# A fused attention and two-MLP kernel: wo's whole weights in three buffers, late conversions a step earlier, GpSimd's subtractions on VectorE

## The chip, the cores and the metric

The kernel runs on one core of one Trainium2 chip. The metric is the device time of one execution in microseconds, the median of several runs. TensorE (PE) does the matmuls, VectorE (DVE) and ScalarE (ACT) the elementwise work, GpSimd (POOL) a few subtractions, and SyncE (SP) issues nearly all DMAs.

## The reference

Three stages, all in float32:

```
attention   4 x 8 heads, 768 positions, 64 wide, in chunks of 32 queries:
            softmax(0.125 * q k^T) v over 8 memory keys, 16 to the left, the chunk, 8 to the right
moe         x = heads side by side (3072 x 512);  x = ((x @ w_a) * (x @ w_b)) @ w_out     d_ff 1536
moe2        h = x @ w_in (1024 wide);  solu = h * softmax(h)
            ln = (solu - mean) / sqrt(var + 1e-6) * g_ln;  result = ln @ w_out
```

The weights of both MLPs arrive as 64-bit floats and are turned into 32-bit ones on the chip.

## The kernel before, in words

**Products.** Every float32 value is split into a high part in the fast 32-bit format and a low part, and a product is three matmuls (low by high, high by low, high by high). So for each operand ScalarE copies the high part and VectorE subtracts it from the value to get the low part (`op_hi` and `op_lo`, line 691, for operands of the third products; `w2_hi` and `w2_lo`, line 816, for the second MLP's weights; `x1_hi` and `x1_lo`, line 575; `h_hi` and `h_lo`, line 927). Many products are done by a seven-product scheme (Strassen-Winograd's), which needs sums and differences of blocks of weights and of inputs (`s1_sums`, `wo_sums`, `t1_sum`, `t_sum`, `w2_sub`, `h_sums`).

**Order of time.** The 3072 tokens are six blocks of 512. (1) Block 0: attention, and conversion of the first MLP's weights; (2) block 1, with the attention of later blocks between; the weights' high and low parts and sums go to DRAM (`wsa`, `wsb` for the gates, `wod` for halves of w_out, `woz` for its whole values). (3) Two super-blocks of two blocks each (`sb` 0 and 1): a loop over 12 units `f` of d_ff, seven products a step, with ring buffers for `wsa` and `wsb` (`ring_load`), and then 36 *third products* (`third`), which multiply by pieces of w_out of 256 KB, six of them held at a time (`piece_load`, line 660). (4) The second MLP in 12 pairs of tiles of 128 tokens (`h_...`, `soft_...`, `t_mm`, `o_mm`).

**What sets the order.** TensorE, VectorE and ScalarE run in the order in which the program is written. Work beside the products is put at ticks: `at(t, fn, ...)` files a call, and each product ends with `tick()`, which makes the calls filed for it. `when(sb, f, k)` is the tick of product `k` in step `f`; `f = NF1` (12) is the stretch of third products. The orders of SyncE's and GpSimd's queues are made by the framework's planner from its own simulation; each queue then waits in order, so an instruction that waits holds up all behind it.

**Around the change.** Whole values of w_out (`woz`) are loaded for each of six pairs `p` of units into `wo_z()`, two rows of one tile (`r[3][:, 4:6]`, the same rows for all six), turned into sums (`wo_sums`), split (`wo_hi`, `wo_lo`) and stored as `wos` (`wo_store`, line 629); `wo_load` is line 615. The first two weights' whole values and their DRAM copies come from `wo_keep` (the addition is line 477). The last heads' attention runs in *pairs* of 128 queries between the products of super-block 0: `pair_load` (lines 288 and 292) loads values, q and k, `pair_S` makes scores, `pair_V` (line 360) the value products after a copy on ScalarE (line 345). In super-block 1 the 16 units of the second MLP's weights are loaded, converted (`w2_load`, `w2_abs`, `w2_low`, `w2_range`, `w2_sign`, `w2_add`), and split; seven of w_out's eight units are stored and placed again later (`w2_store`, `w2_place`); the w_in units are combined by `w2_sub` on GpSimd (line 824) in the stretch of third products. `h_sums` (line 901, GpSimd) makes the sums of a tile pair's inputs. Results of the first MLP go to DRAM by `out3` and `out3x` (lines 732 and 737).

The lines that give the shared tile and GpSimd's subtraction:

```
    def wo_z():
        return held["r"][3][:, 4:6]
...
        nc.gpsimd.tensor_tensor(out=w2_z(o), in0=w2_z(a), in1=w2_z(b), op=ALU.subtract)
```

Of the kernel before, what the change touches and what calls it, by code (L numbers as in the profile page):

```python
# [8 lines left out]
F32 = mybir.dt.float32  # L9
# [46 lines left out]
def fused_kernel(  # L56
# [552 lines left out]

    def wo_z():  # L610
        return held["r"][3][:, 4:6]

    def wo_load(p):
        for i in range(2):
            nc.sync.dma_start(wo_z()[:, i], woz[p + i * HF])

    def wo_sums():
        z = flat(wo_z()).rearrange("p (i c) -> p i c", i=4)
        for o, a, b, op in (
            (3, 1, 3, ALU.add),  # L620
            (1, 0, 1, ALU.subtract),
            (0, 3, 0, ALU.subtract),
            (2, 2, 0, ALU.subtract),
        ):
            nc.vector.tensor_tensor(out=z[:, o], in0=z[:, a], in1=z[:, b], op=op)

    def wo_store(p, h):
        t = flat(wo_z() if h else chunk(14).bitcast(F32))
        nc.sync.dma_start(wos[p][:, h].rearrange("p n c -> p (n c)"), t)

    def wo_hi(p):
        nc.scalar.copy(flat(chunk(14)), flat(wo_z()))

    def wo_lo(p):
        z = flat(wo_z())
# [12 lines left out]
    def piece_load(q):  # L648

        i, p = (0, q) if q < HF else order[q - HF]  # L650
        src = {
            0: lambda: wod[p][:, :, 0:256],
            1: lambda: wod[p + HF][:, :, 0:256],
            2: lambda: wos[p][:, :, 0],
            3: lambda: wos[p][:, :, 3],
            4: lambda: wos[p][:, :, 2],
            5: lambda: wos[p][:, :, 1],
            6: lambda: wod[p + HF][:, :, 256:512],
        }[i]()
        nc.sync.dma_start(wo_piece(q).bitcast(F32), src)  # L660

    def op_chunk(k):

        if k < 0:
            return chunk(27 + (k + HF) % 2)
        if k < 24:
            n = (17, 20, 27, 29, 15, 16, 21, 18, 19, 22, 23, 28)[k % 12]
        else:
            n = ((17, 20, 27, 29, 18, 19, 23, 28), (17, 20, 27, 29, 21, 22, 23, 28))[cur["sb"]][k % 8]
        return chunk(n)  # L670
# [218 lines left out]
    def h_sums(j):  # L889
# [5 lines left out]
        for i, a, b, op in (  # L895
# [508 lines left out]
    for t, i in zip((17, 20, 22, 25, 27, 29, 32), (0, 1, 2, 5, 3, 4, 6)):  # L1404
        at(when(0, NF1, t - 2), x1_hi, i)
        at(when(0, NF1, t), x1_lo, i)
    for sb in range(NSB):
        for p in range(HF):
# [3 lines left out]
            if p < HF - 1:  # L1412
# [17 lines left out]
            ),  # L1430
        )[sb]
        for p in range(HF):
            a, b = order.index((2, p)), order.index((1, p))
            for (f, k), (fn, *i) in zip(places[p], (
                (t_sum, 2, p), (op_hi, a), (op_hi, b), (op_lo, a), (op_lo, b), (t_sum, 4, p)
            )):
                at(when(sb, f, k), fn, *i)
        for p in range(HF):
            at(when(sb, NF1, 8 + p), t_sum, 3, p)
        for k in range(12, 6 * HF):  # L1440
            at(when(sb, NF1, k - 6), op_hi, k)
            at(when(sb, NF1, k - 5), op_lo, k)

    at(when(1, 0, 0), w2_buffers)
    for i in range(16):
        s = i // 3 * 2 + (1, 1, 2)[i % 3]
        for f, k, fn, *a in (
            ((s - 2, 5) if i > 2 else (0, i)) + (w2_load, w2_unit(i), i % 3),
            (s - 1, 4 if s > 1 else 5, w2_abs, i % 3, i), (s - 1, 4 if s > 1 else 5, w2_low, i % 3),
            (s, (0, 3, 0)[i % 3], w2_range, i), (s, (1, 4, 1)[i % 3], w2_sign, i % 3, i),  # L1450
            (s, (1, 4, 1)[i % 3], w2_add, i % 3, i),
            *(((s, (5, 6, 5)[i % 3], w2_hi, 14 + i, i), (s + 1, 1, w2_lo, 14 + i, i)) if i < 8 else ()),
            *(((s + 1, 3, w2_store, 14 + i),) if i < 7 else ()),
        ):
            at(when(1, f, k), fn, *a)
    for k in range(2):
        t, z = 13 * k, 8 + 4 * k
        for n, fn, *a in (
            (0, w2_hi, k, z), (0, w2_hi, 4 + k, z + 3), (1, w2_hi, 2 + k, z + 2),
            (1, w2_lo, k, z), (2, w2_lo, 4 + k, z + 3), (3, w2_lo, 2 + k, z + 2),  # L1460
            (4, w2_sub, z, z + 1, z), (5, w2_sub, z + 1, z + 3, z + 1),
            (6, w2_sub, z + 3, z + 3, z), (7, w2_sub, z + 2, z + 2, z + 3),
            (6, w2_hi, 6 + k, z), (7, w2_hi, 10 + k, z + 1), (8, w2_hi, 8 + k, z + 3), (9, w2_hi, 12 + k, z + 2),
            (8, w2_lo, 6 + k, z), (9, w2_lo, 10 + k, z + 1), (10, w2_lo, 8 + k, z + 3), (11, w2_lo, 12 + k, z + 2),
        ):
            at(when(1, NF1, t + n), fn, *a)
    for t, fn, *i in (
        (8, h_load, 0), (9, h_load, 1), (12, h_sums, 0), (14, h_buffers), (24, h_load, 2), (24, h_sums, 1),
        *((30 + n, w2_place, 14 + n, c) for n, c in enumerate((21, 22, 23, 28))),
        *((15 + 3 * n, h_hi, 0, n) for n in range(3)), *((16 + 3 * n, h_lo, 0, n) for n in range(3)),  # L1470
    ):
# [30 lines left out]
    for sb in range(NSB):  # L1502
# [6 lines left out]
        for f in range(NF1):  # L1509
# [5 lines left out]
            if g == 0:  # L1515
# [246 lines left out]
```

## Time and profile before

| | |
|---|---|
| runs | 925.69, 926.03, 927.2 us; median 926.03 |
| profiled execution | 925.9 us, its span 924.1 us |
| PE (matmul) | 883.6 us busy, 96% of the span, 6864 instructions |
| PE weight loads | 728.8 us, 79% |
| DVE | 686.3 us, 74% |
| ACT | 400.9 us, 43% |
| POOL | 80.1 us, 9% |
| DMA | 189.86 MB, mean 205 GB/s |

A busy PE is not a PE at its peak, since matmuls overlap and their ends are modelled; the count of matmuls in a stretch tells more. The chain of work that ended last is 70% PE and 18% DVE. The granted clock is TensorE's, as a share of 2.4 GHz; 0.50 is 1.2 GHz.

### The profile page before, as it was taken

How to read it: one execution, taken by the hardware profiler on the slowest of the kernel's cores; microseconds unless marked ns; L12 is line 12 of the kernel's file. 1: busy time of each engine (PE TensorE's matmuls, PEld its weight loads, DVE VectorE, ACT ScalarE, POOL GpSimd, SP SyncE). 2: the span in 40 equal slices, each digit the busy share in tenths (PEclk: the TensorE clock that was granted, in tenths of full speed). 3: DMA queues.
4: the chain of work that ended last, by engine and by line, in shares of the span. 5: the costliest groups of instructions: out<-in, count | busy, mean ns of one | idle time of the engine just before them, and what ended most of it. 6: DMA issues, size and time to landing. Idle time of an engine off the chain costs nothing.

```text
span 924.1 us, 16906 instructions
## 1 busy us (share of the span) xinstructions
PE 883.6 (96%) x6864; PEld 728.8 (79%) x6864; DVE 686.3 (74%) x1129; ACT 400.9 (43%) x587; POOL 80.1 (9%) x89
## 2 busy tenths in 40 slices
PE   4899999999999999799999999988999999999998
PEld 3788877887888888687788888866887888888887
DVE  6999956878877576469937878898588666666661
ACT  3777633334343232235635553465334444444331
POOL 0000000000000000000000000126232222220000
PEclk9999999999999999899999999999999999999999
DMA  9999655769858888646998988355612111100001
GB/s 372 420 411 338 229 177 202 251 225 311 271 156 333 300 276 317 227 149 193 298 369 282 334 320 284 107 180 179 242 35 70 46 52 62 48 29 29 24 23 46
DMA packets 85694, 189.86 MB, mean 205 GB/s; under 512 B 6640, under 2 KB 56048, under 8 KB 81136
## 3 DMA queue, kind: packets, MB, share of 16 engines
q1 hardware_dynamic: 85584, 188.77, 57.9%
q8 instruction: 54, 0.88, 0.4%
q14 instruction: 24, 0.20, 0.1%
q0 software_dynamic: 32, 0.00, 0.0%
HBM read 134.75 MB, written 54.00 MB: 204 GB/s over the span
## 4 chain that ended last, share of the span: by engine, by line
PE 70%; DVE 18%; issue 4%; DMA 4%; ACT 1%; POOL 1%; SPq 1%; DVEq 0%; ACTq 0%; POOLq 0%
PE acc L745 24%; PE acc L950 9%; PE pab L1120 4%; PE pab L1121 4%; PE pab L1119 4%; PE pab L716 4%; PE pab L840 2%; PE acc L716 2%; PE pab L841 2%; PE pab L842 2%; DVE Z L406 2%; PE pst L1101 2%; DVE Z L398 2%; DVE w L691 2%; PE px L360 2%
## 5 line engine op out<-in xcount | busy, mean ns | idle before, releaser
L745 PE MATMUL acc<-w 128*128 128x512 f32 x978 | 229.6, 393 | 0.0
L745 PEld LDWEIGHTS acc<-w 128*128 128x128 f32 x978 | 184.0, 189 | 38.6
L901 POOL TENSOR_TENSOR w2ld<-w2ld 128x256 f32<-128x256 f32 x48 | 44.1, 940 | 558.0 <-ACT w L812 465.3
L716 PE MATMUL pab<-w 128*128 128x512 f32 x288 | 71.6, 392 | 9.2 <-DVE w L691 7.3
L840 PE MATMUL pab<-x,w 128*128 128x512 f32 (+1 forms) x200 | 79.5, 397 | 0.9 <-ACT x L272 0.9
L841 PE MATMUL pab<-x,w 128*128 128x512 f32 (+1 forms) x200 | 77.6, 388 | 0.1
L842 PE MATMUL pab<-x,w 128*128 128x512 f32 (+1 forms) x200 | 77.4, 387 | 0.0
L1120 PE MATMUL pab<-w 128*128 128x512 f32 (+1 forms) x200 | 76.2, 381 | 0.7 <-DVE w L1107 0.7
L1119 PE MATMUL pab<-w 128*128 128x512 f32 (+1 forms) x200 | 76.5, 382 | 0.0
L1121 PE MATMUL pab<-w 128*128 128x512 f32 (+1 forms) x200 | 76.3, 381 | 0.0
L1107 DVE TENSOR_TENSOR w<-pst,w 128x1024 fp32r<-128x1024 f32 x24 | 29.1, 1213 | 58.4 <-ACT w L1106 58.3
L716 PEld LDWEIGHTS pab<-w 128*128 128x128 f32 x288 | 53.5, 188 | 23.1 <-DVE w L691 9.5
L758 DVE TENSOR_TENSOR part<-acc,part 128x512 f32<-128x512 f32 x56 | 38.6, 690 | 39.6 <-PE acc L745 24.0
L950 PE MATMUL acc<-w 128*128 128x512 f32 x252 | 61.6, 394 | 0.5 <-ACT part L962 0.5
L950 PE MATMUL acc<-w,hx 128*128 128x512 f32 x252 | 61.5, 394 | 0.1
L950 PEld LDWEIGHTS acc<-w 128*128 128x128 f32 x252 | 46.4, 188 | 10.2 <-ACT part L962 0.9
L950 PEld LDWEIGHTS acc<-w,hx 128*128 128x128 f32 x252 | 46.6, 188 | 9.9 <-DVE mx L966 0.5
L716 PE MATMUL acc<-w 128*128 128x512 f32 x216 | 52.2, 390 | 0.0
L716 PEld LDWEIGHTS acc<-w 128*128 128x128 f32 x216 | 40.4, 188 | 9.1 <-DVE w L691 0.5
L840 PEld LDWEIGHTS pab<-x,w 128*128 128x128 f32 x200 | 38.5, 193 | 8.9 <-ACT x L272 1.2
L842 PEld LDWEIGHTS pab<-x,w 128*128 128x128 f32 x200 | 38.5, 193 | 7.6
L841 PEld LDWEIGHTS pab<-x,w 128*128 128x128 f32 x200 | 38.6, 193 | 7.5 <-DVE x L277 0.4
(237 smaller groups left out, 1593.6 us busy)
## 6 DMA issues: line engine op xcount, KB each, us to landing
w<-wsa SPq DMA_DIRECT2D x24, 1024.0 KB, 7.0
w<-wsb SPq DMA_DIRECT2D x24, 768.0 KB, 7.0
raw<-w1d_dram SPq DMA_DIRECT2D x11, 1536.0 KB, 21.7
qk<-qkv_dram SPq DMA_DIRECT2D x20, 640.0 KB, 6.2
w<-wos SPq DMA_DIRECT2D x48, 256.0 KB, 3.6
v<-qkv_dram SPq DMA_DIRECT2D x20, 512.0 KB, 5.4
w<-wod SPq DMA_DIRECT2D x36, 256.0 KB, 5.0
wsa<-w SPq DMA_DIRECT2D x24, 256.0 KB, 3.9
```

Of the source, the lines that this page charges most:

```text
L716: nc.tensor.matmul(ps, w[:, u, sl], g[:, v], start=first and n == 0, stop=last and n == 2, skip_group_check=True,)
L745: nc.tensor.matmul(ps, w[:, u, k], xx[v][:, k], start=(start and k == 0 and i == 0), stop=(stop and k == 1 and i == 2), skip_group_check=True,
L758: nc.vector.tensor_tensor(out=o, in0=a, in1=b, op=op)
L840: nc.tensor.matmul(ps, wl, xh, start=first, stop=False)
L841: nc.tensor.matmul(ps, wh, xl, start=False, stop=False)
L842: nc.tensor.matmul(ps, wh, xh, start=False, stop=last)
L901: nc.gpsimd.tensor_tensor(out=s4[:, i], in0=a, in1=b, op=op)
L950: nc.tensor.matmul(ps, x, y, start=(start and k == 0 and i == 0), stop=(stop and k == 1 and i == 2), skip_group_check=True,)
L1107: last = nc.vector.tensor_tensor(out=ll, in0=pt, in1=lh.bitcast(F32), op=ALU.subtract)
L1119: nc.tensor.matmul(po, s["lh"][:, f], wl, start=(f == 0), stop=False)
L1120: nc.tensor.matmul(po, s["ll"][:, f], wh, start=False, stop=False)
L1121: nc.tensor.matmul(po, s["lh"][:, f], wh, start=False, stop=(f == NF2 - 1))
```

## The change

- `wo_z(p)` gives one of three places; loads of the whole weights, their sums and stores stand at other ticks.
- `wod` and `wos` are laid out so that a piece is one run of 2 KB per partition; `wo_keep` stores in two halves; weights 6 get their whole values stored from the conversion itself, and the `wo_keep` calls move.
- In super-block 0 the list of operand places is eight long from product 12 on, and the ring loads for super-block 1's first two units move.
- Results are stored a tick after they are computed (`x2_store`).
- The second MLP's conversions begin a step earlier, three w_in units go through DRAM, the eighth w_out unit too; `w2_sub` runs on VectorE, and `h_sums` does for the first pair of tiles.
- `t_sum` 3 of super-block 1 moves into the loop; some `op_lo` come a tick later; `x1` operand 6 goes ahead of 4; loads and sums of the first tiles come later.

```diff
-    wod = [dram.tile([P, 2, WC], F32, name=f"wod{f}") for f in range(NF1)]
+    wod = [dram.tile([P, 2, 2, 256], F32, name=f"wod{f}") for f in range(NF1)]
-    wos = [dram.tile([P, 2, 4, 256], F32, name=f"wos{p}") for p in range(HF)]
-    w2s = [dram.tile([P, 2, WC], F32, name=f"w2s{i}") for i in range(NF2 - 1)]
+    wos = [dram.tile([P, 4, 2, 256], F32, name=f"wos{p}") for p in range(HF)]
+    w2s = [dram.tile([P, 2, WC], F32, name=f"w2s{i}") for i in range(NF2 + 3)]
...
-        if f > HF:
+        if f >= HF:
             nc.sync.dma_start(woz[f], zs[f][0][:, 2 * WC:3 * WC])
...
-        nc.sync.dma_start(wod[f], w)
-        if f <= HF:
+        for a in range(2):
+            nc.sync.dma_start(wod[f][:, a], w[:, :, 256 * a:256 * a + 256])
+        if f < HF:
...
-    def wo_z():
-        return held["r"][3][:, 4:6]
+    def wo_z(p):
+        if p % 3 == 0 or p == 5:
+            return held["r"][3][:, 4:6]
+        return held["r"][4][:, 4 - p // 2 % 2 * 2:][:, 0:2]
...
-        if k < 24:
+        if k < (12, 24)[cur["sb"]]:
             n = (17, 20, 27, 29, 15, 16, 21, 18, 19, 22, 23, 28)[k % 12]
...
+            n = (17, 20, 27, 29, 18, 19, 23, 28)[(k - 12) % 8]
...
-        nc.sync.dma_start(x2d[NDIR + 2 * cur["sb"] + half][:, d], t)
+        at(clock + 1, x2_store, 2 * cur["sb"] + half, d, t)
...
-        nc.gpsimd.tensor_tensor(out=w2_z(o), in0=w2_z(a), in1=w2_z(b), op=ALU.subtract)
+        nc.vector.tensor_tensor(out=w2_z(o), in0=w2_z(a), in1=w2_z(b), op=ALU.subtract)
...
-            nc.gpsimd.tensor_tensor(out=s4[:, i], in0=a, in1=b, op=op)
+            (nc.gpsimd if j else nc.vector).tensor_tensor(out=s4[:, i], in0=a, in1=b, op=op)
...
-        at(3 + 6 * f, wo_keep, f)
+        at((0, 0, 14, 14, 14, 32, 38, 44, 48, 52, 56, 60)[f], wo_keep, f)
...
+        f0 = 2 * p - p // 5
         for f, k, fn, *i in (
-            (0, 5, wo_load, p), (1, 4, wo_sums), (1, 6, wo_hi, p),
-            (2, 1, wo_store, p, 0), (2, 1, wo_lo, p), (2, 2, wo_store, p, 1),
+            ((0, 1, 2, 3, 6, 9)[p], 2, wo_load), (f0 + 1, 4, wo_sums), (f0 + 1, 6, wo_hi),
+            (f0 + 2, 1, wo_store, 0), (f0 + 2, 1, wo_lo), (f0 + 2, 2, wo_store, 1),
         ):
-            at(when(0, 2 * p + f, k), fn, *i)
+            at(when(0, f, k), fn, p, *i)
...
-        for p in range(HF):
-            at(when(sb, NF1, 8 + p), t_sum, 3, p)
+        for p, (f, k) in enumerate((
+            [(NF1, 8 + p) for p in range(HF)],
+            ((9, 5), (10, 2), (10, 4), (10, 5), (11, 1), (NF1, 7)),
+        )[sb]):
+            at(when(sb, f, k), t_sum, 3, p)
         for k in range(12, 6 * HF):
             at(when(sb, NF1, k - 6), op_hi, k)
-            at(when(sb, NF1, k - 5), op_lo, k)
+            at(when(sb, NF1, k - 4 - (k > 15)), op_lo, k)
...
-        s = i // 3 * 2 + (1, 1, 2)[i % 3]
+        s = i // 3 * 2 + i % 3 // 2
...
+        (6, 5, w2_hi, 0, 8), (7, 1, w2_lo, 0, 8), (7, 3, w2_store, 0),
+        (7, 5, w2_hi, 4, 11), (8, 0, w2_lo, 4, 11), (8, 2, w2_store, 4),
+        (8, 5, w2_hi, 2, 10), (9, 1, w2_lo, 2, 10), (9, 3, w2_store, 2),
+        (9, 4, w2_sub, 8, 9, 8), (9, 4, w2_sub, 9, 11, 9), (10, 1, w2_sub, 11, 11, 8), (10, 4, w2_sub, 10, 10, 11),
...
+            (12, w2_sub, 12, 13, 12), (15, w2_sub, 13, 15, 13), (16, w2_sub, 15, 15, 12), (17, w2_sub, 14, 14, 15),
...
+            (14, h_buffers), (8, h_load, 0), (9, h_load, 1), (22, h_sums, 0), (32, h_load, 2), (32, h_sums, 1),
...
-        if sb == 0 and k in (18, 22, 29, 30):
-            ring_load(NF1 + k // 29, k in (22, 30))
+        if sb == 0 and k in (8, 12, 34):
+            ring_load(NF1 + k // 34, k == 12)
...
+            if g == NF1:
+                ring_load(NF1 + 1, 1)
             s_product(x, g, 0, 2, 2, False, False)
```

## Rows read from the trace of the kernel before

**Rows 1.** Windows of 20 us: length, engines' busy us (count), clock, DMA share, GB/s.
```profile
380.00:400.00 20.00, 14.14 (x115) 11.59 (x114) 9.72 (x16) 3.75 (x5) 0.00 (x0) 0.83 0.61 205
...
440.00:460.00 20.00, 18.65 (x83) 15.13 (x82) 20.00 (x28) 12.99 (x20) 0.00 (x0) 1.00 0.93 298
...
480.00:500.00 20.00, 20.00 (x90) 16.54 (x90) 15.98 (x27) 11.66 (x21) 0.00 (x0) 1.00 0.79 265
...
600.00:620.00 20.00, 16.52 (x71) 12.69 (x70) 19.93 (x27) 13.13 (x24) 6.52 (x4) 1.00 0.54 172
620.00:640.00 20.00, 16.62 (x71) 12.76 (x69) 17.64 (x24) 11.78 (x21) 16.03 (x8) 1.00 0.46 145
640.00:660.00 20.00, 19.42 (x86) 16.09 (x87) 10.77 (x18) 5.98 (x11) 1.48 (x3) 1.00 0.95 320
```

**Rows 2.** TensorE's waits, whole span: who waited for whom, total us, times, longest.
```profile
PE pab L716 <- DVE w L691: 7.3, 4, 2.3
PE s L193 <- DMA qk<-qkv_dram: 5.9, 1, 5.9
...
PE pab L716 <- DMA w<-wos: 1.8, 2, 1.4
PE px L360 <- ACT EB L345: 1.6, 2, 1.4
```

**Rows 3.** Windows with GpSimd busy: PE, PEld, DVE, ACT, POOL as in rows 1.
```profile
594.20:598.40 4.20, 4.20 (x21) 3.46 (x20) 4.17 (x5) 1.03 (x2) 4.09 (x4) 1.00 0.39 118
...
600.90:607.70 6.80, 4.61 (x21) 3.50 (x20) 6.80 (x5) 5.05 (x11) 6.51 (x4) 1.00 0.55 174
...
631.30:640.00 8.70, 5.46 (x23) 3.86 (x21) 7.54 (x8) 7.47 (x14) 8.41 (x7) 1.00 0.25 79
```

**Rows 4.** Line 691 on VectorE: shortest, median, longest in ns; first and last start.
```profile
L691 DVE TENSOR_TENSOR w<-r,w x56: 675/684/1774, 296.6 to 645.3; 128x512 fp32r<-128x512 f32 x56
```

**Rows 5.** Windows of the second super-block's last four steps, as in rows 1.
```profile
555.07:564.59 9.52, 9.52 (x43) 7.89 (x42) 6.32 (x11) 3.69 (x7) 0.00 (x0) 1.00 0.82 293
564.59:574.11 9.52, 9.52 (x43) 7.88 (x42) 9.06 (x16) 4.20 (x8) 0.00 (x0) 1.00 0.75 255
574.11:583.63 9.52, 9.52 (x43) 7.89 (x42) 6.33 (x11) 3.69 (x7) 0.00 (x0) 1.00 0.57 204
583.63:593.15 9.52, 9.52 (x43) 7.88 (x42) 8.89 (x15) 4.01 (x9) 0.00 (x0) 1.00 0.16 54
```

**Rows 6.** SyncE's waits in 360 to 400 us.
```profile
SPq L615 <- DMA wos<-r: 6.3, 1, 6.3
```

**Rows 7.** Timeline 374 to 392 us: start, us, instruction, idle before it and releaser.
```profile
374.20 2.07 PE L360 MATMUL px<-EB,v 64*64 64x32 f32 x128
...
379.02 0.38 SPq L292 DMA_DIRECT2D qk<-qkv_dram  x1
...
385.88 1.16 PE L193 MATMUL s<-qk 64*32 64x64 f32 x64 [5.86 <-DMA qk<-qkv_dram]
```

**Rows 8.** Fine windows after the wait for q and k, as in rows 1.
```profile
385.80:388.90 3.10, 3.02 (x69) 2.50 (x70) 1.70 (x2) 0.00 (x0) 0.00 (x0) 0.50 0.71 287
388.90:392.00 3.10, 3.10 (x11) 2.48 (x10) 1.95 (x3) 0.59 (x1) 0.00 (x0) 0.68 0.04 15
```

**Rows 9.** Line 292, all sixteen loads of q and k.
```profile
DMA to landing us min/median/max: 3.8/6.2/9.9
```

**Rows 10.** DMAs issued 445.2 to 446.2 us: count, KB each, us to landing.
```profile
w<-wsa SPq DMA_DIRECT2D x1, 1024.0 KB, 8.0
```

**Rows 11.** Line 660, SyncE's time to issue a piece: shortest, median, longest in ns.
```profile
L660 SPq DMA_DIRECT2D w<-wos x48: 517/518/577, 306.8 to 630.8; - x48
```

**Rows 12.** Line 477, the additions of `wo_keep`, in ns.
```profile
L477 DVE TENSOR_TENSOR wz<-w x7: 683/684/685, 162.8 to 218.7; 128x512 f32<-128x512 f32 x7
```

**Rows 13.** DMAs issued 464.2 to 465.5 us, as in rows 10.
```profile
w<-wsb SPq DMA_DIRECT2D x1, 768.0 KB, 9.7
```

**Rows 14.** SyncE's waits in 470 to 590 us.
```profile
SPq L821 <- DVE w2x L816: 17.9, 4, 4.5
```

More of the change, by code (lines that the diff above doesn't have):

```diff
@@ L608, in spare, with wo_sums @@
         return EB[:, 0] if p in (3, 5) else AT[:, :]
[L610 to L611 removed]
+    def wo_z(p):
+        if p % 3 == 0 or p == 5:
+            return held["r"][3][:, 4:6]
+        return held["r"][4][:, 4 - p // 2 % 2 * 2:][:, 0:2]
     def wo_load(p):
         for i in range(2):
[L615 to L618 removed]
+            nc.sync.dma_start(wo_z(p)[:, i], woz[p + i * HF])
+    def wo_sums(p):
+        z = flat(wo_z(p)).rearrange("p (i c) -> p i c", i=4)
         for o, a, b, op in (
@@ L627, in wo_store @@
     def wo_store(p, h):
-        t = flat(wo_z() if h else chunk(14).bitcast(F32))
-        nc.sync.dma_start(wos[p][:, h].rearrange("p n c -> p (n c)"), t)
+        t = flat(wo_z(p) if h else chunk(14).bitcast(F32))
+        nc.sync.dma_start(wos[p][:, :, h], t.rearrange("p (n c) -> p n c", n=4))
     def wo_hi(p):
-        nc.scalar.copy(flat(chunk(14)), flat(wo_z()))
+        nc.scalar.copy(flat(chunk(14)), flat(wo_z(p)))
     def wo_lo(p):
-        z = flat(wo_z())
+        z = flat(wo_z(p))
         nc.vector.tensor_tensor(
@@ L651, in piece_load @@
         src = {
[L652 to L658, printed above, removed]
+            0: lambda: wod[p][:, 0],
+            1: lambda: wod[p + HF][:, 0],
+            2: lambda: wos[p][:, 0],
+            3: lambda: wos[p][:, 3],
+            4: lambda: wos[p][:, 2],
+            5: lambda: wos[p][:, 1],
+            6: lambda: wod[p + HF][:, 1],
         }[i]()
@@ L736, in out3x @@
         nc.scalar.copy(t, cur["x", m])
-        nc.sync.dma_start(x2d[NDIR + 2 * cur["sb"] + 1][:, m], t)
+        at(clock + 1, x2_store, 2 * cur["sb"] + 1, m, t)
     def s_product(ps, g, part, a, x, start, stop):
@@ L762, in w2_buffers, with w2_raws @@
     def w2_buffers():
-        held["ld"] = [ld_tile(2 * WC, "w2ld") for _ in range(3)]
         held["x2"] = x_tile(0, F32, "w2x")
         held["z2"] = x_tile(1, F32, "w2z")
+    def w2_raws():
+        held["ld"] = [ld_tile(2 * WC, "w2ld") for _ in range(3)]
     def w2_z(i):
@@ L799, in w2_unit, with w2_spot, w2_row @@
         return win2[r * P:(r + 1) * P, h * WC:(h + 1) * WC]
-    def w2_spot(i):
-        if i % 3 == 1:
+    def w2_spot():
+        n = next_of("spot", 3)
+        if n == 1 or n == 2 and len(w2_dst) >= 8:
             return chunk(14)
-        return held["x2"][:, i % 3:i % 3 + 2].bitcast(F32R)
+        return held["x2"][:, n:n + 2].bitcast(F32R)
+    def w2_row(name):
+        return w2s[name - 14 if name >= 14 else NF2 + name // 2]
     def w2_hi(name, n):
-        w2_dst[name] = chunk(name) if name < 14 else w2_spot(n)
+        w2_dst[name] = w2_spot() if name >= 14 or name in (0, 2, 4) else chunk(name)
         if name >= 14:
@@ L900, in h_sums, with x2_store @@
         ):
-            nc.gpsimd.tensor_tensor(out=s4[:, i], in0=a, in1=b, op=op)
+            (nc.gpsimd if j else nc.vector).tensor_tensor(out=s4[:, i], in0=a, in1=b, op=op)
+    def x2_store(i, d, t):
+        nc.sync.dma_start(x2d[NDIR + i][:, d], t)
     def h_buffers():
@@ L1396, in fused_kernel @@
     for p in range(HF):
+        f0 = 2 * p - p // 5
         for f, k, fn, *i in (
-            (0, 5, wo_load, p), (1, 4, wo_sums), (1, 6, wo_hi, p),
-            (2, 1, wo_store, p, 0), (2, 1, wo_lo, p), (2, 2, wo_store, p, 1),
+            ((0, 1, 2, 3, 6, 9)[p], 2, wo_load), (f0 + 1, 4, wo_sums), (f0 + 1, 6, wo_hi),
+            (f0 + 2, 1, wo_store, 0), (f0 + 2, 1, wo_lo), (f0 + 2, 2, wo_store, 1),
         ):
-            at(when(0, 2 * p + f, k), fn, *i)
+            at(when(0, f, k), fn, p, *i)
     for n, t in enumerate((2, 4, 14, 19)):
         at(when(0, NF1, t), t1_sum, n)
-    for t, i in zip((17, 20, 22, 25, 27, 29, 32), (0, 1, 2, 5, 3, 4, 6)):
+    for t, i in zip((17, 20, 22, 25, 27, 29, 32), (0, 1, 2, 5, 3, 6, 4)):
         at(when(0, NF1, t - 2), x1_hi, i)
@@ L1445, in fused_kernel, with w2_when @@
+    def w2_when(f, k):
+        return when(1, f, k) if f >= 0 else when(0, NF1, 29 + k)
+    at(when(0, NF1, 30), w2_raws)
+    at(when(0, NF1, 33), w2_buffers)
     for i in range(16):
-        s = i // 3 * 2 + (1, 1, 2)[i % 3]
+        s = i // 3 * 2 + i % 3 // 2
         for f, k, fn, *a in (
-            ((s - 2, 5) if i > 2 else (0, i)) + (w2_load, w2_unit(i), i % 3),
-            (s - 1, 4 if s > 1 else 5, w2_abs, i % 3, i), (s - 1, 4 if s > 1 else 5, w2_low, i % 3),
+            ((s - 2, 5) if i > 2 else (-1, 1 + i // 2)) + (w2_load, w2_unit(i), i % 3),
+            (s - 1, 5, w2_abs, i % 3, i), (s - 1, 5, w2_low, i % 3),
@@ L1450, in fused_kernel @@
             (s, (0, 3, 0)[i % 3], w2_range, i), (s, (1, 4, 1)[i % 3], w2_sign, i % 3, i),
             (s, (1, 4, 1)[i % 3], w2_add, i % 3, i),
-            *(((s, (5, 6, 5)[i % 3], w2_hi, 14 + i, i), (s + 1, 1, w2_lo, 14 + i, i)) if i < 8 else ()),
-            *(((s + 1, 3, w2_store, 14 + i),) if i < 7 else ()),
-        ):
[L1455 to L1470, printed above, removed]
+            *(((s, (5, 6, 5)[i % 3], w2_hi, 14 + i, i), (s + 1, 1, w2_lo, 14 + i, i),
+               (s + 1, 3, w2_store, 14 + i)) if i < 8 else ()),
+        ):
+            at(w2_when(f, k), fn, *a)
@@ new lines, in fused_kernel @@
+    for f, k, fn, *a in (
+        (6, 5, w2_hi, 0, 8), (7, 1, w2_lo, 0, 8), (7, 3, w2_store, 0),
+        (7, 5, w2_hi, 4, 11), (8, 0, w2_lo, 4, 11), (8, 2, w2_store, 4),
+        (8, 5, w2_hi, 2, 10), (9, 1, w2_lo, 2, 10), (9, 3, w2_store, 2),
+        (9, 4, w2_sub, 8, 9, 8), (9, 4, w2_sub, 9, 11, 9), (10, 1, w2_sub, 11, 11, 8), (10, 4, w2_sub, 10, 10, 11),
+        *((12, k, fn, *a) for k, fn, *a in (
+            (0, w2_hi, 6, 8), (0, w2_hi, 10, 9), (2, w2_hi, 8, 11), (3, w2_hi, 12, 10),
+            (2, w2_lo, 6, 8), (2, w2_lo, 10, 9), (5, w2_lo, 8, 11), (5, w2_lo, 12, 10),
+            (1, w2_place, 0, 0), (2, w2_place, 4, 4), (3, w2_place, 2, 2),
+            (6, w2_hi, 1, 12), (7, w2_hi, 5, 15), (8, w2_hi, 3, 14),
+            (9, w2_lo, 1, 12), (10, w2_lo, 5, 15), (11, w2_lo, 3, 14),
+            (12, w2_sub, 12, 13, 12), (15, w2_sub, 13, 15, 13), (16, w2_sub, 15, 15, 12), (17, w2_sub, 14, 14, 15),
+            (14, w2_hi, 7, 12), (17, w2_hi, 11, 13), (18, w2_hi, 9, 15), (19, w2_hi, 13, 14),
+            (18, w2_lo, 7, 12), (19, w2_lo, 11, 13), (20, w2_lo, 9, 15), (21, w2_lo, 13, 14),
+            (14, h_buffers), (8, h_load, 0), (9, h_load, 1), (22, h_sums, 0), (32, h_load, 2), (32, h_sums, 1),
+            *((30 + n, w2_place, 14 + n, c) for n, c in enumerate((21, 22, 23, 28))), (20, w2_place, 21, 14),
+            *((t, h_hi, 0, n) for n, t in enumerate((24, 25, 27))), *((t, h_lo, 0, n) for n, t in enumerate((26, 28, 30))),
+        )),
@@ L1471, in fused_kernel @@
     ):
-        at(when(1, NF1, t), fn, *i)
+        at(w2_when(f, k), fn, *a)
     def third(k):
@@ L1602, in fused_kernel @@
     third(35)
+    tick()
     h_a1x(0)
```

8 lines of the change are left out of this document (4 added, 4 removed), and 4 rows, old and new, of the table places.

## The prediction, made before the changed kernel ran

> **What bounds the kernel now.** I read the busy shares first, then the table of 20 us windows, then who TensorE waited for, and last the places of those waits in the order of time. TensorE does the same matmuls before and after, so only time in which it stands can go. From about 40 us on it runs at its own pace, 90 matmuls of 512 columns in 20 us, 0.222 us each, as in 480 to 500 us; the reader is to see which windows fall short of that: 380 to 400 (also a granted clock of 0.83), 440 to 460, 600 to 620, 620 to 640 and 640 to 660 [rows 1]. The list of TensorE's waits gives the four causes that the edits can touch: 7.3 us on VectorE's low-part subtractions of the operands (line 691), 5.9 us on one load of q and k, 1.8 us on loads of wo pieces, 1.6 us on ScalarE's copy before the value products of a pair (line 345) [rows 2].
>
> **1. GpSimd's subtractions go to VectorE.** In 600 to 640 us VectorE is busy 37.6 of 40 us and TensorE waits for it [rows 1]. VectorE is slow there in a special way: while GpSimd is busy, 5, 5 and 8 of its instructions take 4.17, 6.80 and 7.54 us [rows 3], where one of this form has a median of 0.684 us, and the longest took 1.774 [rows 4]. At 0.684 these 18 would be 12.3 us instead of 18.5, so 6.2 us of VectorE's time go to the overlap. After the change eight subtractions of the second weight run on VectorE, and four small ones of the first tile's sums; only the later tiles' sums stay on GpSimd. What VectorE does in the stretch of the 36 third products: it loses five sums of `t_sum` and three low parts, which move ahead of it, and gets four of the eight subtractions and the four of 256 columns. The count is even, the 6.2 us are gone, and each operand's low part is due four or five products before its use (a product is six matmuls, a step of the loop is seven products in 9.52 us [rows 5], so 1.36 us each and 5.4 to 6.8 in all). So TensorE's wait goes. Its price: at least the 7.3 us [rows 2], at most what the three windows lack, (90-71) + (90-71) + (90-86) = 42 matmuls x 0.222 = 9.3 us [rows 1]. I take 8.3.
>
> The Trainium skill (SBUF — State Buffer, "SBUF: two separate sides") has VectorE with two inputs in SBUF and a GpSimd instruction lock each other out for a whole instruction. By that rule each of the four sums that stay on GpSimd for the second tile takes a slot from VectorE for certain; counted in full, at the upper end of term 5, the sum would be 912.5. The rows above agree with such a lock.
>
> What moves ahead lands in the last four steps of the loop of the second super-block. Those steps take 9.52 us of TensorE each; VectorE had 11, 16, 11 and 15 instructions in them, in the second 9.06 us, and TensorE lost no matmul (43 in each) [rows 5]. With conversions one step earlier (one less in these four steps: four instructions off), and four subtractions, five sums and two low parts on top, the 53 become 60, about 15 a step. None passes the 16 that already fit, so I cost this at nothing; if the cover goes, about 2 us.
>
> **2. Three places for wo's whole weights.** In 360 to 400 us SyncE stood 6.3 us in one wait of `wo_load` for the store of the weights before it, because both use the same tile [rows 6]. Behind it in the same queue stands the pair's q and k load. Its buffer was free when the first half of the value products (374.20, 2.07 us long) had run, about 375.3; it went out at 379.02, when that wait was over, and the scores that need it began at 385.88 [rows 7]. TensorE stood 5.9 us for it [rows 2], and then ran at the lower of its two levels: the granted clock is 0.50 from 385.8 to 388.9 and 0.68 from there to 392, so 1.2 GHz until about 390.9 [rows 8], and the 3.9 us of matmuls in it cost half of that, 1.9. The place is worth 7.8 us. After the change the load of weights 4 stands three steps earlier, in another tile, so the q and k load can go out at about 375.5. Landing takes 3.8, 6.2 or 9.9 us (least, median, most) [rows 9]: it lands at 379.3, 381.7 or 385.4, and is wanted at about 380.0 (385.88 less 5.86). The wait left is 0, 1.7 or 5.4. The two loads of whole weights that went out just ahead of it are no longer there, so I take a value below the median, 1.0, with no fall of the clock: gain 6.8, between 2.4 and 7.8.
>
> **3. wo pieces.** The two waits on pieces are 1.8 us. One is for weights 5, whose conversion now ends a step earlier, so it goes. The other follows a ring load: the ring part took 8.0 us to land [rows 10], the pieces behind it in the queue land after it, and a piece is issued only six products ahead, 6 x 1.36 = 8.2 us. The ring loads come ten products earlier, into chunks that the shorter list of operand places leaves free; the same pile can arise there, beside fewer stores. I leave 0.5 of it: gain 1.3, between 0 and 1.8. The store of results waits a tick, which only lets pieces pass.
>
> A piece in runs of 2 KB: SyncE takes 0.52 us to issue one [rows 11], and 0.38 for the q and k load with one run per partition [rows 7]; one is issued every 1.36 us, so that is not on the path and I count nothing. The Trainium skill (DMA: Bandwidth & Descriptors, "Specifications") puts full rate at runs of 512 B and over, which speaks against this edit: by it, too, the gain is nothing. No run here shows a piece in 2 KB runs yet.
>
> **4. Sums of the whole weights at other ticks.** Seven additions of 0.684 us (line 477) stand at VectorE [rows 12]. The seventh goes, since weights 6 are stored straight from the conversion, and the others move to ticks just before a gate, where VectorE waits for TensorE. The 1.6 us on line 345 [rows 2] are VectorE's backlog in front of a value product; two additions less in it would take 1.4 off, none 0. I take 0.8.
>
> **5. What is new.** For the second super-block's second unit the ring parts are issued later: the first after third product 33, the second in the block itself. The first is then wanted two third products and five of the block later, 7 x 1.36 = 9.5 us; a part loaded at this place took 9.7 to land [rows 13]. So from 0 to 0.2 us late, plus what SyncE is held by loads of the second MLP's weights before it; up to 3. I take 0.5. For the four sums still on GpSimd, which now come eight products later, beside VectorE's last low parts or behind them: 0 to 4 x 0.684 = 2.7, I take 0.5. For eight more transfers of 512 KB (four stores, four placements) in stretches that move little: 0 to 1, I take 0.5. Together 1.5, between 0 and 6.
>
> **Sum.** 8.3 + 6.8 + 1.3 + 0.8 = 17.2 off, 1.5 on: the span goes from 924.1 to 908.4. The profiled execution took 925.9, 1.8 more than its span, and stands 0.1 below the median of 926.03: 908.4 + 1.8 + 0.1 = 910.3 us.
>
> **Rivals.** (A) VectorE stays the bound behind the loop: it is full there, and takes over work; the lost time was its amount, not the overlap. For it: 37.6 of 40 us busy. Against it: the lengthened instructions stand only beside GpSimd's. Then term 1 gives about 1: 917.6. (B) The q and k load does not go out earlier, because SyncE's order is planned and something else stands ahead of it, or it lands as late as the slowest one. Term 2 is nothing: 917.1. Both together: 924.4, almost no change; that is also the case in which the change does not do what it says. (C) Slower: SyncE is held in the loop of the second super-block. Before, its stores of second weights waited 17.9 us for VectorE in 4 waits, 4.5 the longest [rows 14], and ring parts stand behind them. A step is 9.5 us and a ring part takes about 7 to land (8.0 in [rows 10]), so a hold of over 2.5 us makes TensorE stand. The change adds stores there and fills VectorE, on which they wait. With 4.5 us at each of eight steps TensorE loses 2.0 and, where its clock falls as after the q and k wait, about 1 more: 8 x 3 = 24, which gives 934. It decides once most holds pass 2.5 us. Against it: holds of 4.5 cost no matmul between 480 and 500.
>
> **Chances.** Forecast 60% (905 to 915: all terms at their full size and nothing new gives 924.1 - 9.3 - 7.8 - 1.8 - 1.4 + 1.9 = 905.7), A 15%, B 12%, A and B or a new wait of some 6 us 5%, C 8%. The range for 8 in 10 takes in A and B: 904.5 to 920.5; the forecast's own is 905 to 915. A measurement of this kernel tells 0.2%, 1.9 us, from no change. Faster by more than that: 0.60 + 0.15 + 0.12 + half of the 5% and a little of C, 0.90; within it 0.03; slower 0.07.
>
> **What would show it.** Term 1: no GpSimd work from line 824, VectorE's instructions at 0.68 us throughout the third products, 88 or more matmuls in each such 20 us. Term 2: no wait of SyncE on line 615, the last pair's q and k load issued within 1 us of the first value products, no granted clock of 0.50 near it. Term 3: no wait of TensorE on wo pieces over 0.5 us. Term 4: line 345's wait under 1 us. Wrong it is if TensorE waits for ring parts or for the loads of the second weights at the start of the second super-block, if waits on line 691 stay, or if VectorE's backlog in the last four steps makes TensorE stand.

## The result and the profile after

The changed kernel takes 918.76 us (median of 4 runs, 916.97 to 919.06) against 925.86 us for the kernel before (4 runs, 925.02 to 927.2): ratio 0.9918, 95% interval 0.9901 to 0.9935, so 7.1 us faster where 15.6 were forecast. Its profiled execution took 919.06 us, with a span of 917.3. TensorE is busy for the same 883 us; GpSimd falls from 80.1 to 57.6 us.

Windows of the changed kernel (length, busy us of PE, PEld, DVE, ACT, POOL with counts, granted clock, DMA share, GB/s), against [rows 1]:

```profile
80.00:100.00 20.00, 17.75 (x76) 13.83 (x75) 16.39 (x15) 11.46 (x11) 0.00 (x0) 1.00 0.77 260
380.00:400.00 20.00, 15.22 (x209) 12.27 (x203) 9.07 (x14) 6.07 (x9) 0.00 (x0) 0.83 0.64 225
440.00:460.00 20.00, 19.99 (x89) 16.27 (x88) 19.55 (x28) 14.73 (x23) 0.00 (x0) 1.00 0.74 248
...
600.00:620.00 20.00, 20.00 (x90) 16.58 (x89) 19.77 (x34) 12.84 (x24) 0.00 (x0) 1.00 0.64 217
620.00:640.00 20.00, 20.00 (x89) 16.55 (x89) 16.85 (x29) 13.85 (x26) 3.10 (x4) 1.00 0.72 231
640.00:660.00 20.00, 19.88 (x88) 16.13 (x87) 10.03 (x21) 6.89 (x11) 3.32 (x4) 1.00 0.75 271
```

The first line has no answer among the rows of before, so here is the same window of the kernel before:

```profile
80.00:100.00 20.00, 20.00 (x90) 16.57 (x89) 19.93 (x18) 14.18 (x14) 0.00 (x0) 1.00 0.77 277
```

Three things are to be seen. The third products of the second super-block run at TensorE's own pace, as forecast. The window with the q and k load is still short and its clock still averages 0.83. And in 80 to 100 us, which no step of the prediction mentions, 14 matmuls are gone. TensorE's waits of the changed kernel, against [rows 2]:

```profile
PE s L193 <- DMA qk<-qkv_dram: 4.8, 1, 4.8
...
PE acc L851 <- ACT gh L868: 1.2, 1, 1.2
PE px L360 <- ACT EB L345: 1.1, 2, 0.9
PE pab L851 <- DVE w L413: 1.0, 2, 0.8
```

The 7.3 us on the low parts are gone, the q and k load still costs 4.8 us, in place of 5.9, and the first MLP has new waits (lines 851 and 868 are 840 and 857 of before). The balance in order of time, from the profiled executions: the last pair's first value products start at 378.40 us, 4.2 later than in [rows 7]; the scores behind the q and k load at 388.98, 3.1 later; the end of the span is 6.8 earlier. So 4.2 us are lost ahead of that load, 1.1 gained at it, and 9.9 behind it. The 14 matmuls, at 0.222 us each, are 3.1 of the 4.2; what makes up the rest was not traced (the granted clock in 140 to 160 us averages 0.86, and 0.91 before).

**The loss in the first MLP.** Weights 6, 7 and 8 are single units of d_ff here; weights 3, 4 and 5, further down, are pairs of units, the `p` of `wo_load`. ScalarE's and SyncE's timeline of the changed kernel (start, us, engine, line, instruction, idle before it and its releaser):

```profile
80.93 0.56 ACT L1264 COPY G<-pab 128x512 f32<-128x512 f32 x1
81.92 1.48 SPq L473 DMA_DIRECT2D wod<-w  x2
83.50 0.65 SPq L451 DMA_DIRECT2D woz<-Z  x1
87.41 1.58 ACT L377 ACTIVATE Z<-raw 128x1536 f32<-128x1536 f32 x1 [5.92 <-DMA woz<-Z]
```

Line 451 is the new direct store of weights 6 out of the conversion's own tile. Weights 8 are converted in the same half of that tile; their first instruction (line 377) was ready at 81.5 us and waited for the store, which was issued at 83.50 and landed 3.8 us later. VectorE was done with weights 6 at 77.90; the store stood behind other stores that SyncE issued without a break from 78.16 on. In the kernel before, that instruction started at 81.52 and the first such store, of weights 7, went out at 86.29.

**The q and k load.** The changed kernel's timeline at the place of [rows 7]:

```profile
375.61 0.52 SPq L632 DMA_DIRECT2D wos<-r  x1
378.40 2.07 PE L360 MATMUL px<-EB,v 64*64 64x32 f32 x128
382.20 0.79 SPq L618 DMA_DIRECT2D r<-woz  x2
383.09 0.38 SPq L292 DMA_DIRECT2D qk<-qkv_dram  x1
388.98 1.16 PE L193 MATMUL s<-qk 64*32 64x64 f32 x64 [4.78 <-DMA qk<-qkv_dram]
```

and SyncE's wait in 360 to 400 us, which answers to [rows 6]:

```profile
SPq L618 <- DMA wos<-r: 6.0, 1, 6.0
```

The wait of `wo_load` that was to go is still there, with other weights: the load at 382.20 is that of weights 5. They use the place of weights 3, so they wait for the store of weights 3 issued at 375.61, and the q and k load stands behind them.

SyncE issues a wo piece in 0.32 us now, against [rows 11]; line 663 on SyncE (shortest, median, longest in ns):

```profile
L663 SPq DMA_DIRECT2D w<-wos x48: 319/320/422, 311.3 to 628.4; - x48
```

TensorE's waits in 412 to 475 us, where the kernel before lost 1.8 us on pieces, are 0.4 on ScalarE's copy of an operand and 0.4 on a piece:

```profile
PE pab L721 <- ACT w L692: 0.4, 1, 0.4
PE acc L721 <- DMA w<-wod: 0.4, 1, 0.4
```

### The profile page after: what moved, and what is told of

Read it like the earlier page. It is cut to its first block, busy times and chain, and to the rows that moved or that the text cites. A ratio compares the mean times of both kernels' runs of the same rounds, so it can differ in the third digit from the quotient of the medians.

```text
span 917.3 us, 16924 instructions
## 1 busy us (share of the span) xinstructions
PE 883.2 (96%) x6864; PEld 729.5 (80%) x6864; DVE 684.1 (75%) x1140; ACT 400.4 (44%) x587; POOL 57.6 (6%) x77
## 4 chain that ended last, share of the span: by engine, by line
PE 76%; DVE 12%; issue 5%; DMA 4%; ACT 2%; SPq 0%; POOL 0%; ACTq 0%; DVEq 0%; POOLq 0%
PE acc L750 23%; PE acc L964 10%; PE pab L721 7%; PE acc L721 5%; PE pab L1134 4%; PE pab L1135 4%; PE pab L1133 4%; PE pab L851 3%; PE pab L852 2%; PE pab L853 2%; PE pst L1115 2%; DVE Z L398 2%; DVE Z L406 2%; PE px L360 2%; PE s L193 2%
## 5 line engine op out<-in xcount | busy, mean ns | idle before, releaser
L912 POOL TENSOR_TENSOR w2ld<-w2ld 128x256 f32<-128x256 f32 x44 | 39.1, 910 | 589.0 <-PE pab L721 502.1
```

The costliest lines, as they stand in the source:

```text
L912: (nc.gpsimd if j else nc.vector).tensor_tensor(out=s4[:, i], in0=a, in1=b, op=op)
```

## The experiments

Three questions: whether the store of weights 6 makes the loss in the first MLP, whether weights 5 keep the q and k load late, and what took the waits on the low parts away. Ratios are to the kernel before, timed on the same chip, with 95% intervals.

**1. Weights 6 as before** (the conditions of `w1_add`, the direct store, and of `wo_keep`, the sum).

```diff
-        if f >= HF:
+        if f > HF:
...
-        if f < HF:
+        if f <= HF:
```

> The changed kernel with weights 6 treated as before: their middle third is summed at VectorE in the keep step, not stored straight from the conversion. Theory S (this store costs time: the next conversion's absolute values on ScalarE overwrite the tile and wait 5.9 us for the store): ScalarE's wait near 87 us and TensorE's standing at 88.3, 90.1 and 93.1 us (1.2, 0.2, 0.8) go, 80 to 100 us holds 90 matmuls again in place of 76, and 3 to 4 us come off: 914.8 to 915.8. Rival Q (SyncE's queue is held by the twice as many stores of the middle thirds, and any store there would have waited): the waits move to the next store, under 1.5 us off, 917.3 to 918.8.

Measured 916.12 us, 0.9902 (0.9879 to 0.9925): 2.6 off by the medians, with an interval that overlaps that of the changed kernel, so the times of this run alone do not show a gain. The trace is plainer; the first row is the window, the second ScalarE's instruction, the third a wait of TensorE:

```profile
80.00:100.00 20.00, 20.00 (x90) 16.57 (x89) 19.93 (x18) 14.07 (x14) 0.00 (x0) 1.00 0.82 276
...
81.56 1.64 ACT L377 ACTIVATE Z<-raw 128x1536 f32<-128x1536 f32 x1 [0.58 <-DVE w L413]
...
PE acc L750 <- DMA w<-wsa: 1.3, 1, 1.3
```

All 90 matmuls are back, and TensorE is done in front of the q and k load at 381.33 us instead of 384.20, 2.9 earlier, after giving 1.3 of it to a ring part near 287. By the trace theory S holds at that place; the time came out 0.3 above its range. With the seventh addition back, the wait on line 345 near 220 us is 1.4 again (0.9 without it).

**2. The middle thirds stored in one transfer, as before** (and their pieces read in runs of 1 KB; the lines that do so are left out below).

```diff
-    wod = [dram.tile([P, 2, 2, 256], F32, name=f"wod{f}") for f in range(NF1)]
+    wod = [dram.tile([P, 2, WC], F32, name=f"wod{f}") for f in range(NF1)]
...
-        for a in range(2):
-            nc.sync.dma_start(wod[f][:, a], w[:, :, 256 * a:256 * a + 256])
+        nc.sync.dma_start(wod[f], w)
...
```

> The changed kernel with the middle thirds of wo stored as before, in one 512 KB transfer, their pieces read in runs of 1 KB again. Theory S (the store of weights 6 itself): ScalarE still waits about 5 us near 87 us, 918.0 to 919.0, no change. Rival Q (the doubled stores hold SyncE): the store of weights 6 goes out 1.4 us or more earlier, ScalarE's wait falls below 3.5 us, and 1.5 to 3 us come off: 915.8 to 917.3. Runs of 1 KB instead of 2 KB cost nothing by both: issue 0.52 us in place of 0.33, one every 1.36 us.

Measured 917.38 us, 0.9908 (0.9885 to 0.9932), not told apart from the changed kernel, and between the ranges of S and Q. SyncE's store of weights 6 and ScalarE's instruction behind it:

```profile
82.00 0.61 SPq L451 DMA_DIRECT2D woz<-Z  x1
...
86.06 1.58 ACT L377 ACTIVATE Z<-raw 128x1536 f32<-128x1536 f32 x1 [4.89 <-DVE Z L406]
```

The store goes out 1.5 us earlier (the trace names a VectorE instruction that was long done as releaser; the store landed 4.0 us after its issue, at 86.0, where the wait ends). So the doubled stores hold it, as rival Q says, but only 1.0 of the 5.9 us goes. The rest of the wait stays: the data were ready at 77.60, SyncE had other stores to issue for 4.4 us, and landing took 4.0 more. Unforeseen, 2.5 us of waits for pieces come up between 436 and 471 us; run 9 asks whether the 1 KB runs make them.

**3. Weights 5 loaded by GpSimd's queue.**

```diff
-            nc.sync.dma_start(wo_z(p)[:, i], woz[p + i * HF])
+            (nc.gpsimd if p == 5 else nc.sync).dma_start(wo_z(p)[:, i], woz[p + i * HF])
```

> The changed kernel with the two loads of whole wo weights 5 issued by GpSimd instead of SyncE: their wait for the store out of the same place then stands in another queue than the q and k load of the last pair. Theory H (the place that is still shared by weights 3 and 5, hoisted ahead of the q and k load in SyncE's queue, keeps it late): the q and k load goes out at about 376 to 377 instead of 383.1, TensorE's wait for it falls from 4.8 us to under 1.5, the granted clock stays above 0.9 in 380 to 400, and 4.5 to 6.5 us come off: 912.3 to 914.3. Rival L (the load's landing, not its issue, is late: whole weights are still on the way in front of it): it goes out earlier but lands after 382, the wait stays above 2.5 us, 0 to 2.5 us off: 916.3 to 918.8.

Measured 912.32 us, 0.9858 (0.9832 to 0.9884): 6.4 us faster than the changed kernel. Timeline:

```profile
378.44 2.07 PE L360 MATMUL px<-EB,v 64*64 64x32 f32 x128
...
379.63 0.33 SPq L292 DMA_DIRECT2D qk<-qkv_dram  x1
...
382.73 1.14 POOL L618 DMA_DIRECT2D r<-woz  x2 [250.04 <-DMA wos<-r]
...
385.27 0.84 PE L193 MATMUL s<-qk 64*32 64x64 f32 x64 [1.03 <-DMA qk<-qkv_dram]
```

The load of weights 5 still waits until 382.7, but nothing stands behind it. The q and k load goes out when the first half of the value products has freed its buffer, 1.2 us after they began, lands in 5.6 us, and TensorE waits 1.03 us. The granted clock stays at 1.00 in 380 to 400 us. That is theory H, with its time and its wait; only the issue is later than the 376 to 377 us that it had named, 1.2 us after value products that start at 378.44. (Another wait of 1.1 us for a q and k load is new at 321 us.)

**4. Weights 5 in the other place instead** (loaded two steps earlier into the third place, converted ahead of weights 4; every load on SyncE).

```diff
-        if p % 3 == 0 or p == 5:
+        if p % 3 == 0:
-        return held["r"][4][:, 4 - p // 2 % 2 * 2:][:, 0:2]
+        return held["r"][4][:, (4, 2)[p in (2, 5)]:][:, 0:2]
-        f0 = 2 * p - p // 5
+        f0 = (0, 2, 4, 6, 8, 7)[p]
-            ((0, 1, 2, 3, 6, 9)[p], 2, wo_load), ...
+            ((0, 1, 2, 3, 6, 7)[p], 2, wo_load), ...
```

> The changed kernel with weights 5 in the third place, free at that time, and loaded two steps earlier, before weights 4 are converted; all loads stay on SyncE. Theory H (the place shared by weights 3 and 5 makes the wait that stands in front of the q and k load, whichever queue holds it): SyncE has no wait of wo_load left near 376, TensorE's wait for q and k falls from 4.8 us to under 2, 4 to 6.5 us off: 912.3 to 914.8, as with GpSimd's queue. Rival N (only another queue helps, because the two loads now stand in front of the pair before and make it late there): 1 to 3 us of wait appear near 320, 915 to 917.5.

Measured 912.85 us, 0.9844 (0.9827 to 0.9860): 5.9 off. SyncE's two rows, and TensorE's wait in 300 to 400 us:

```profile
374.09 0.52 SPq L632 DMA_DIRECT2D wos<-r  x1
378.10 0.34 SPq L292 DMA_DIRECT2D qk<-qkv_dram  x1
...
PE s L193 <- DMA qk<-qkv_dram: 1.1, 1, 1.1
```

No wait has appeared near 320 us. Another queue, or another place with an earlier tick, does the same, so the load of weights 5 that waits in SyncE's queue for the place is the cause. Run 4 changes place and tick together and does not part them. The price of the late q and k load is 5.9 to 6.4 us by the medians, 5.6 to 6.9 by the ratios.

**5. The subtractions back on GpSimd, at the new ticks.**

```diff
-        nc.vector.tensor_tensor(out=w2_z(o), ...)
+        nc.gpsimd.tensor_tensor(out=w2_z(o), ...)
-            (nc.gpsimd if j else nc.vector).tensor_tensor(out=s4[:, i], ...)
+            nc.gpsimd.tensor_tensor(out=s4[:, i], ...)
```

> The changed kernel with the eight subtractions of the second weight and the four sums of the first tile back on GpSimd, at the changed kernel's own ticks. Theory O (VectorE's loss was the overlap with GpSimd): VectorE's instructions beside these are lengthened again, waits on the low parts (7.3 us before) come back in 600 to 660, 5 to 9 us more: 924 to 928. Rival M (the gain came from the work that was moved ahead into the last steps of the second super-block, VectorE's amount being the bound): within 2 us of the changed kernel, 917 to 921.

Measured 918.45 us, 0.9923 (0.9901 to 0.9945): no difference from the changed kernel, as rival M had it. My theory O falls in the form in which I put it. VectorE's low parts beside GpSimd are still lengthened; here are six of line 696 in 600 to 645 us, with a mean of 868 ns instead of 684 (busy us, mean ns, idle before):

```profile
L696 DVE TENSOR_TENSOR w<-Z,w 128x512 fp32r<-128x512 f32 x6 | 5.2, 868 | 0.2 <-ACT w L692 0.2
```

but TensorE waits for none of them.

**6. The kernel before with the engines changed alone** (the two edits of run 5 the other way, in the old code).

> The kernel before with only the engines changed: the eight subtractions of the second weight and the four sums of the first tile on VectorE, at their old ticks. Theory O (VectorE's loss was the overlap with GpSimd; either the engines or the order is enough to take the waits away): no lengthened instruction is left in 590 to 645, the waits on the low parts (7.3 us) fall below 2, 5 to 9 us off: 917 to 921. Rival M (the amount of VectorE's work in front of the last third products is what binds, and only moving it ahead helps): 8 x 0.684 + 4 x 0.42 = 7.2 us of work come on for the 6.2 us of lengthening that go, the waits stay between 5 and 9 us: 924 to 928.

Measured 920.74 us, 0.9936 (0.9919 to 0.9954): 6.2 us faster than before, in theory O's range. TensorE's waits on line 691 in 590 to 645 us, 7.3 before, are 2.6, a little above the 2 that theory O allowed:

```profile
PE pab L716 <- DVE w L691: 1.6, 3, 0.8
PE acc L716 <- DVE w L691: 1.0, 1, 1.0
```

**7. The kernel before with the sums of kind 3 moved ahead alone** (the changed kernel's list of their ticks in the old code).

```diff
-            at(when(sb, NF1, 8 + p), t_sum, 3, p)
+            [(NF1, 8 + p) for p in range(HF)],                                # sb 0
+            ((9, 5), (10, 2), (10, 4), (10, 5), (11, 1), (NF1, 7)),           # sb 1
```

> The kernel before with one part of the reordering alone: five of the six sums of kind 3 of the second super-block at the changed kernel's ticks, in the last steps of the loop instead of among the third products. Theory O+ (VectorE is short by a sum of both: each us taken out of the stretch before 640 comes back to TensorE): 5 x 0.684 = 3.4 us of work are gone there, the waits on the low parts fall from 7.3 to about 4, 922 to 923.5. Rival M+ (these sums are what stood in front of the first late operand, and behind them the queue keeps up): waits below 1.5, 918 to 920.5. If VectorE's place of loss lies behind the sums: no gain, 925 to 927.

Measured 928.17 us, 1.0015 (0.9998 to 1.0031): no gain. In 590 to 645 us:

```profile
PE pab L716 <- DVE w L691: 5.2, 3, 2.4
PE pab L716 <- DMA w<-wos: 1.9, 1, 1.9
```

2.1 us of the wait go, and 1.9 come back as a wait for a piece just behind, after which the clock is down (0.83 on average in 640 to 660 us). What the sums would be worth without that second wait is not shown.

**8. The changed kernel with both undone**: the engines, and the five sums back among the third products.

> The changed kernel with two parts undone together: the eight subtractions and the four sums of the first tile on GpSimd again, and the five sums of kind 3 back among the third products; only the conversions and subtractions of the second MLP's weights keep their earlier ticks. Measured with the engines undone alone: 918.5. If the sums that were moved ahead carried the gain there: waits on the low parts of 3 to 7 us come back in 600 to 645, 921 to 926. If the earlier ticks of the conversions and subtractions carry it: 918 to 919.5, with waits below 1 us.

Measured 917.15 us, 0.9896 (0.9879 to 0.9913), so again no loss. The two windows, and GpSimd's longest subtraction:

```profile
600.00:620.00 20.00, 20.00 (x90) 16.53 (x89) 19.93 (x34) 13.46 (x25) 9.88 (x2) 1.00 0.64 216
620.00:640.00 20.00, 20.00 (x90) 16.57 (x89) 18.32 (x24) 13.28 (x25) 8.24 (x7) 1.00 0.73 237
...
612.94 8.34 POOL L835 TENSOR_TENSOR EB<-r,EB 128x512 f32<-128x512 f32 x1
```

VectorE is busy 38.25 of 40 us, more than the 37.6 of [rows 1], GpSimd overlaps it for 18 us, and TensorE loses nothing. So neither the engines nor the sums are needed: what is left of the reordering is enough. The earlier ticks of the second MLP's conversions and subtractions are its main part, but the few other ticks that moved with them were not undone by themselves, so it is not shown that these ticks alone are enough.

**9. The repairs together.** Runs 1 and 3; these with the edit of run 2; and runs 1 and 4:

> The changed kernel with the two repairs together: weights 6 summed and stored as before, weights 5 loaded by GpSimd. Alone they took the changed kernel's 918.8 to 916.1 and to 912.3. If they add up (the losses lie in different stages): 918.8 - 2.7 - 6.4 = 909.7, between 908.5 and 911.0. If the time that the first stage gets back is lost again (the operands of the second weight then wait for ring parts near 287 us, as 1.3 us with the first repair alone): 911.0 to 912.5.

> The two repairs together, as measured at 910.0, and besides the middle thirds of wo stored in one transfer and read in runs of 1 KB, as before. Theory R (the 2 KB runs are worth the loss that came up with the 1 KB runs in the changed kernel: 2.5 us of waits for pieces near 437 and 469 where the changed kernel has 0.4 for each engine): 911 to 912.5. Rival Z (these waits shift from kernel to kernel with the order of the queue and not with the runs): 909.3 to 910.7.

> The changed kernel with weights 6 summed and stored as before and weights 5 in the third place, loaded two steps earlier by SyncE: the two repairs, the second by its other way. If place and queue are worth the same: 909.3 to 911.0. If the earlier load costs the pair before: 911.5 to 914.

Measured 910.04 us, 0.9822 (0.9803 to 0.9841); 911.23 us, 0.9822 (0.9806 to 0.9839); and 909.47 us, 0.9815 (0.9799 to 0.9831). The repairs add up, and the last version beats both kernels, by 17.2 us the one before. The repair of weights 6 is worth nearly the same wherever it is added (918.8 to 916.1, 912.3 to 910.0, 912.9 to 909.5): 2.3 to 3.4 us by the medians, 1.5 to 3.3 by the ratios. The intervals of each pair overlap, but the three agree. On the 1 KB runs the second version settles nothing: its ratio is that of the first, as rival Z has it, its median lies in theory R's range, and its trace has 2.1 us of waits for pieces in 412 to 475 us where the first has 0.6. What such runs cost stays open. Windows of the third:

```profile
80.00:100.00 20.00, 20.00 (x90) 16.53 (x90) 19.93 (x18) 14.23 (x13) 0.00 (x0) 1.00 0.80 272
380.00:400.00 20.00, 18.56 (x146) 15.52 (x147) 15.57 (x23) 7.06 (x11) 0.00 (x0) 1.00 0.83 284
600.00:620.00 20.00, 20.00 (x90) 16.57 (x89) 18.97 (x34) 14.16 (x26) 0.00 (x0) 1.00 0.69 218
```

## Why the prediction missed

**Term 2 is the step that failed**: "The two loads of whole weights that went out just ahead of it are no longer there." I followed weights 4 out of the shared place and not weights 5, which still use it and whose load the change moves from step 10 of the loop to step 9, into the very gap. Forecast 6.8 us; by the traces 1.1 came at the wait itself and the clock fell again. It is the mechanism of rival B, to which I gave 12%. The rest of the step was right: with weights 5 out of the way, by place or by queue, the load leaves when its buffer is free, TensorE waits 1.03 or 1.1 us (runs 3 and 4) where I had taken 1.0, and the clock does not fall. In run 9 the wait is 1.5 to 1.83, and in one version of three the clock falls, so there was some luck in 1.0 and no fall. The repairs gave the missing 5.9 to 6.4 us.

**An edit costed at nothing was the second error**: in term 4, "the seventh goes, since weights 6 are stored straight from the conversion." I counted the addition that it saves and not the store that it adds, which reads a tile that the conversion two weights later overwrites. The place has no slack: in 80 to 100 us of the kernel before VectorE is busy 19.93 and TensorE 20.00 of 20 us, so what ScalarE waits there comes through. The price is 2.3 to 3.4 us by the medians (run 9). The saved addition did what was said, the waits on line 345 falling from 1.6 to 1.1 us: 0.5 for 0.8. The two runs of each stored middle third belong to it: they hold SyncE, and the store went out 1.5 us later for it (run 2).

**Term 1 came in size, and for a reason that I had only half.** The waits are gone, and what was gained behind the q and k load, 9.9 us, is about what I had summed there (8.3 for this term, 1.3 for pieces). But I gave it to the engines alone and costed the moved work at nothing. Each is enough, or nearly, by itself: engines alone 6.2 us (run 6), the order without the engines all of it (runs 5 and 8). The lock that the prediction cites from the Trainium skill (SBUF — State Buffer, "SBUF: two separate sides") shows from both sides in these traces. VectorE's instructions are lengthened to some 1.77 us beside GpSimd's, as in [rows 3]. But in run 8 GpSimd's subtraction of 8.34 us was the one that stood, and VectorE's of 128x512 beside it took 0.68 each.

The windows of [rows 3] leave out the same thing in the kernel before: GpSimd's subtraction at 623.63 us, beside which VectorE's of 128x512 took no longer than alone. It is part of what TensorE waited for, and not by way of VectorE's length:

```profile
623.63 7.62 POOL L824 TENSOR_TENSOR EB<-EB 128x512 f32<-128x512 f32 x1 [15.92 <-DVE w L816]
...
631.29 0.62 ACT L812 CAST w<-EB 128x512 fp32r<-128x512 f32 x1 [5.48 <-POOL EB L824]
...
632.46 0.72 DVE L691 TENSOR_TENSOR w<-r,w 128x512 fp32r<-128x512 f32 x1 [2.35 <-ACT w L687]
...
636.61 1.66 PE L716 MATMUL pab<-w 128*128 128x512 f32 x6 [1.51 <-DVE w L691]
...
640.58 2.79 PE L716 MATMUL pab<-w 128*128 128x512 f32 x11 [2.31 <-DVE w L691]
```

ScalarE's next instruction needed the result and stood 5.48 us for it; the operand's copy behind it in ScalarE's order came late, VectorE stood 2.35 us for that copy, and two of TensorE's four waits follow; the chain of work that ended last runs through these rows. In run 7, where the waits stayed, ScalarE still stands 4.5 us for this subtraction; in run 8, where they are gone, 0.65 us for one of 8.34, since the copy that needs it stands later in ScalarE's order. Run 6 takes away this dependence together with the lengthening, so what each was worth is not shown. Rival A (the amount, not the overlap) is no better: VectorE was busier in run 8 than before and nothing was late. What decides is the instruction that stands in front of an operand's copy or low part when it falls due: the trace shows it for these two waits; for the other two it is argued.

**Term 3** came to about 1.0 of 1.3 us (0.4 on a piece and 0.4 on a copy left in place of 1.8). **Term 5** cost nothing that the trace shows: no wait for a ring part of the second super-block's second unit, and only 0.4 us at the start of that super-block, on a ScalarE copy. Rival C did not happen: TensorE is busy throughout 500 to 640 us, with 89 or 90 matmuls in each 20.

With both errors mended the three versions of run 9 measured 909.5 to 911.2 us, and the forecast was 910.3; that the other terms' errors (term 5's 1.5 us did not come, terms 3 and 4 gave less) cancel is luck.

## What to carry to other kernels

When a change gives shared buffers new places, list every user of each place after the change, in the order of the queue that loads them: one user left behind kept 4.8 of the 5.9 us of the wait, because what costs is the load queued behind it. An added store from a tile that is soon overwritten is an edit of the path even if it replaces arithmetic; compare its issue and landing with the next write of the tile. And where one cause explains a wait, undo each part of the change by itself in both directions: from the old kernel an engine swap was worth 6 us, from the new one nothing. A slow instruction off the path can also cost through an engine that stands for its result; look at who waits for it, not only at what it slows.

## What was not expected of the hardware

A piece of 256 KB takes SyncE 0.32 us to issue in runs of 2 KB, 0.52 in runs of 1 KB [rows 11]; whether that is worth any time the runs do not show. TensorE's clock after a short wait for q and k went both ways: after 1.03, 1.1, 1.5 and 1.6 us the granted clock was 1.00 in the stretch behind it, after 1.83 us (the first version of run 9) it was 0.70 on average in the next 5.6 us, so partly at 1.2 GHz:

```profile
382.40:388.00 5.60, 5.55 (x78) 4.48 (x79) 3.65 (x4) 0.59 (x1) 0.00 (x0) 0.70 0.72 290
```
